# Attention with a gated unit behind it: the factor leaves the maxima before their transpose and meets them behind it, and products of the same columns are issued apart

## The chip, the cores and the metric

The program runs on one core of a Trainium2 chip, as one launch. The metric is the device time of the launch in microseconds. A core has five engines that work in parallel, each through its own instructions in order: TensorE (PE in the profile; its weight loads are PEld), VectorE (DVE), ScalarE (ACT), GpSimd (POOL) and SyncE (SP), which here issues the transfers between memories. Matrix products are written to PSUM (eight banks of 128 rows by 512 fp32 numbers); everything else lies in SBUF.

## What is computed

The inputs are q, k and v of 8 batches and 8 heads, 1152 positions, 64 numbers a head. Queries are averaged in pairs, so 576 query rows meet 1152 keys. The reference, cut to what matters:

```python
q_pool = q.reshape(B, H, S // 2, 2, D).mean(axis=3)
scores = scale * np.matmul(q_pool, k.transpose(0, 1, 3, 2))
scores = scores - np.max(scores, axis=-1, keepdims=True)
attn = np.exp(scores)
attn = attn / (np.sum(attn, axis=-1, keepdims=True) + 1e-09)
x = np.matmul(attn, v)                       # heads side by side: 512 wide
h = np.maximum(x @ w_in, 0.0)
u, v = h[..., :512], h[..., 512:]            # v is normalised over its row
gated = u * (einsum(w_spatial, normalised v) + b_spatial)
return gated @ w_out
```

## The kernel before

**Numbers in two halves.** Products run on 16-bit numbers, and each fp32 operand is split into a high and a low half, scaled by powers of two (`scales`, lines 340 to 357). A score is `khh` times `qhl` (the high half of k against both halves of q, 128 rows deep) plus `KL` times `X` (the low half of k against the high half of q). `KL` and `X` are 66 rows deep: rows 64 and 65 of `X` hold the row's maximum, as two halves, and those of `KL` hold -2^15, so the second product also takes the maximum off.

**Pairs of heads.** The work goes by 32 pairs of heads. For pair i there are four strands, each written as a generator that stops at `yield`:

- `prep(i)` (line 535) loads and splits q and k. It computes the scales `s` and `r`, from these `esc` (the factor of the exponent, line 551, on ACT) and `lnp` (lines 554 to 558, on DVE): log(64) / ESC times the product of the two scales, cut off at 2^29. `lnp` is the same in all 128 rows, since `scales` sums over the rows with a matrix of ones.
- `maxima(i)` (line 594) multiplies q and k once more for the maxima alone: nine groups of 128 query rows, three products of 384 keys each (line 617, or 608 for the group of tails), and one DVE reduction for each (line 623). Its PSUM banks come from the pool `ps_m` (two banks, tile `pm`), and, while no gated unit is under way, in turn from `ps_w` (tile `pw`).
- `shift` (line 631), twice in each `maxima`, for five groups and for four: the three maxima of a group become one (line 635), `lnp` is taken off (636), the 128 x 5 numbers are transposed by PE into a bank of `ps_m` (640), split into two halves divided by 2^15 (642, 643), and sent by two transfers on SP's queue to the two rows of `X` (648).
- `attention(i)` (line 785) goes through 18 steps. Each makes one tile of 128 keys by 512 query rows: two products (793, 794), the exponent on ACT out of PSUM (799), and on POOL the low half of the result, both in SBUF (811). The exponent is kept as fp32; its upper 16 bits are read as bf16, and the rest is stored over the lower 16 bits as fp16. Two steps later `values` (line 699) multiplies the tile with the values: for each of four blocks of 128 query rows, the upper half times the high half of v with a column of ones (713, 65 columns), the upper half times the low half of v (717, 64 columns, into the first 64 of the same columns), and then four times the rest times the high half (722). `tail_tile` (line 801) does the 64 query rows that are left over for each head: four or five blocks of keys, for each one product of line 793 and one of 794 into the same 64 columns, four tiles for each pair of heads.

**The gated unit.** After every second batch a `gated_unit` (line 831) for 1152 rows runs between the steps of the following pairs; its products are 512 columns wide. The last one runs alone at the end. In the first pairs no unit is there yet, and the weights are loaded and split instead (`load_weights`, line 401).

**The order.** The strands are advanced at fixed rates (lines 1101 to 1120), but this gives only a first order. At the end `Order.pin` (line 183) goes through the whole program with a cost for each instruction (`cost`, line 146), keeps what depends on what, and chooses for each engine which instruction comes next: the one that is ready first by its due time, and of those the earliest written. It also has a term for DVE operations that read only SBUF while POOL works on SBUF (`two_from_sbuf`, line 178): they are taken to wait for each other. The order so found is pinned by a dependency from each instruction to the one before it on its engine. Products into one PSUM tile keep their written order. So an edit of a few instructions can move others.

Of the kernel before, what the change touches and what calls it, by code (L numbers as in the profile page):

```python
# [16 lines left out]
AF = mybir.ActivationFunctionType  # L17
ALU = mybir.AluOpType
# [8 lines left out]
MROW = 2.0 ** 15  # L27

PEXP = 2.0 ** 6
# [232 lines left out]
def attn_sgu_kernel(ctx: ExitStack, tc: tile.TileContext, qT, kT, v, w_in, w_spT, b_sp, w_out, out):  # L262
    nc = tc.nc
    P = 128
# [10 lines left out]
    TAIL = S - MAIN  # L275
    S2 = 2 * S
    NT = S2 // P
    KR = D + 2
    ESC = 0.5 / D ** 0.5
# [85 lines left out]
    def square_sum(acc, src, junk):  # L365
        nc.scalar.activation(junk, src, AF.Square, bias=0.0, scale=1.0, accum_out=acc)
# [168 lines left out]
    def prep(i):  # L535
        st = state[i]
        kt, qt = st["kt"], st["qt"]
        X, KL, khh, qhl = (x[i % NSET] for x in (xq, klo, khi, qhi))
        k0 = kt.rearrange("p (c k) -> p c k", k=P)
        q0, q1 = qt[:, 0:S], qt[:, S:]  # L540
        st.update(qhl=qhl, khh=khh, X=X, KL=KL)
        nc.gpsimd.tensor_add(q0, q0, q1)
        sq = sm.tile([P, 2], F32, name="sq", bufs=2)
        junk = KL[:, 0].rearrange("p c k -> p (c k)")
        square_sum(sq[:, 0:1], kt, junk)
        yield
        square_sum(sq[:, 1:2], q0, junk[:, :S])
        yield
        s, r = yield from scales(sq, "qk", math.log2(ESC) / 2)
        esc = sm.tile([P, 1], F32, name="esc", bufs=NSET)  # L550
        nc.scalar.activation(esc, r[:, 0:1], AF.Copy, bias=0.0, scale=r[:, 1:2])


        lnp = sm.tile([P, 1], F32, name="lnp", bufs=2)
        nc.vector.scalar_tensor_tensor(
            out=lnp, in0=s[:, 0:1], scalar=math.log(PEXP) / ESC, in1=s[:, 1:2], op0=ALU.mult, op1=ALU.mult
        )
        nc.vector.tensor_scalar_min(lnp, lnp, 2.0 ** 29)
        st.update(esc=esc, lnp=lnp)
        s_k, s_q = s[:, 0:1], s[:, 1:2]  # L560
        yield

        lower, upper = slice(0, D), slice(D, P)
        head(X[:, 0], q0, s_q)
        rest(qhl[:, 1], q0, s_q, X[:, 0])
        yield
        nc.sync.dma_start(out=qhl[lower, 0], in_=X[lower, 0])
        nc.sync.dma_start(out=qhl[upper, 0], in_=qhl[lower, 1])
        for h, (a, rows) in enumerate(((MAIN, lower), (0, upper))):
            nc.sync.dma_start(out=qd[i % 2][rows, h], in_=X[rows, 0, a : a + TAIL])  # L570
        kn = st["kn"] = ld.tile([P, NC, P], F16, name="kn")
        for a, z in ((0, 5), (5, NC)):
            if i < 8:
                head(kn[:, a:z], k0[:, a:z], s_k)
                yield
                rest(KL[:, 0, a:z], k0[:, a:z], s_k, kn[:, a:z])
            else:
                nc.scalar.activation(k0[:, a:z], k0[:, a:z], AF.Copy, bias=0.0, scale=s_k)
                yield
                nc.scalar.activation(kn[:, a:z], k0[:, a:z], AF.Copy, bias=0.0, scale=1.0)  # L580
                nc.gpsimd.tensor_sub(KL[:, 0, a:z], k0[:, a:z], kn[:, a:z])
            yield
        nc.sync.dma_start(out=khh[lower, 0], in_=kn[lower])
        nc.sync.dma_start(out=khh[upper, 0], in_=kn[lower])
        nc.sync.dma_start(out=qhl[lower, 1], in_=X[upper, 0])
        nc.sync.dma_start(out=khh[lower, 1], in_=kn[upper])
        nc.sync.dma_start(out=khh[upper, 1], in_=kn[upper])
        nc.sync.dma_start(out=X[lower, 1], in_=X[upper, 0])
        nc.sync.dma_start(out=KL[lower, 1], in_=KL[upper, 0])
        nc.sync.dma_start(out=KL[D:KR, 0], in_=KL[D:KR, 1])  # L590
        yield
# [39 lines left out]
    def shift(st, mt, a, z):  # L631
        X = st["X"]
        n = z - a
        mx = sm.tile([P, NT], F32, name="mx", bufs=2)
        nc.vector.reduce_max(out=mx[:, :n], in_=mt[:, a:z], axis=AX.X)
        nc.vector.tensor_scalar_sub(mx[:, :n], mx[:, :n], st["lnp"])
        yield
        yield
        pt = ps_m.tile([P, 512], F32, name="pm")
        nc.tensor.transpose(out=pt[:n, :P], in_=mx[:, :n], identity=ident)  # L640
        mr = sm.tile([NT, 2, P], F16, name="mr", bufs=2)
        nc.vector.tensor_scalar_mul(mr[:n, 0], pt[:n, :P], 1.0 / MROW)
        nc.vector.scalar_tensor_tensor(
            out=mr[:n, 1], in0=pt[:n, :P], scalar=1.0 / MROW, in1=mr[:n, 0], op0=ALU.mult, op1=ALU.subtract
        )
        for r in range(2):
            rows = X[D + r : D + r + 1].rearrange("p h s -> p (h s)")
            nc.sync.dma_start(out=rows[:, a * P : z * P], in_=mr[:n, r])
        yield
# [3 lines left out]
    TAILS = (slice(MAIN, S), slice(0, TAIL))  # L653
# [45 lines left out]
    def values(i, k):  # L699


        st = state[i]
        h, c = divmod(k, NC)
        if c == 0:
            st["o"] = ps_o.tile([P, MAIN], F32, name="o")
        o = st["o"][:, : 4 * D1].rearrange("p (t d) -> p t d", d=D1)
        pt = st["pt"][k]
        top = pt.bitcast(BF16)[:, 1::2]
        rst = pt.bitcast(F16)[:, 0::2]
        vp = vps[i % 2][:, h, c]  # L710
        for t in range(4):
            cols = slice(t * P, (t + 1) * P)
            nc.tensor.matmul(  # L713
                o[:, t], lhsT=top[:, cols], rhs=vp[:, D : D + D1], start=c == 0 and t == 0, stop=False,
                skip_group_check=True,
            )
            nc.tensor.matmul(  # L717
                o[:, t, 0:D], lhsT=top[:, cols], rhs=vp[:, 0:D], start=False, stop=False, skip_group_check=True
            )
        for t in range(4):  # L720
            cols = slice(t * P, (t + 1) * P)
            nc.tensor.matmul(  # L722
                o[:, t], lhsT=rst[:, cols], rhs=vp[:, D : D + D1], start=False, stop=c == NC - 1,
                skip_group_check=True,
            )
        if c == NC - 1:
            if h == 0:
                st["xm"] = wk.tile([P, 4, P], F32, name="xm")
            r = inverse(o[:, :, D], "den")
            nc.vector.tensor_tensor(  # L730
                out=st["xm"][:, :, h * D : (h + 1) * D], in0=o[:, :, 0:D],
                in1=r.unsqueeze(2).to_broadcast([P, 4, D]), op=ALU.mult,
            )
            if h == 1:
                later.append([2, lambda: turn_main(i)])
# [49 lines left out]
    def attention(i):  # L785

        st = state[i]
        qhl, khh, X, KL, esc = (st[n] for n in ("qhl", "khh", "X", "KL", "esc"))
        ptl = pt_.tile([P, NC, 2, TAIL], F32, name="ptl")
        st.update(ptl=ptl, pt=[])  # L790

        def products(o, c, h, q):
            nc.tensor.matmul(o, lhsT=khh[:, h, c, :], rhs=qhl[:, h, q], start=True, stop=False)  # L793
            nc.tensor.matmul(o, lhsT=KL[0:KR, h, c, :], rhs=X[0:KR, h, q], start=False, stop=True)  # L794

        def main_tile(pt, c, h):
            ps = ps_s.tile([P, MAIN], F32, name="pss")
            products(ps, c, h, MAINS[h])
            nc.scalar.activation(pt, ps, AF.Exp, bias=0.0, scale=esc)  # L799

        def tail_tile(h, n):
            ps = ps_s.tile([P, MAIN], F32, name="pss")
            a, z = CUT[n], CUT[n + 1]
            for c in range(a, z):
                products(ps[:, (c - a) * TAIL : (c - a + 1) * TAIL], c, h, TAILS[h])
            o = ps[:, : (z - a) * TAIL].rearrange("p (c s) -> p c s", s=TAIL)
            nc.scalar.activation(ptl[:, a:z, h], o, AF.Exp, bias=0.0, scale=esc)  # L807

        def split(t):

            nc.gpsimd.tensor_sub(t.bitcast(F16)[..., 0::2], t, t.bitcast(BF16)[..., 1::2])  # L811

        for k in range(STEPS):
            h, c = divmod(k, NC)
            st["pt"].append(pp.tile([P, MAIN], F32, name="pt"))
            main_tile(st["pt"][k], c, h)
            split(st["pt"][k])
            yield
            todo.append((i, k))
            turn()  # L820
            yield
            if k in (1, 2, 3, 4):
                tail_tile((k - 1) % 2, (k - 1) // 2)
                yield
            if k == TAIL_SPLIT:
                split(ptl.rearrange("p c h s -> p c (h s)"))
            if k == TAIL_AT:
                tail_values(i)
# [347 lines left out]
```

## Time and profile before

| | |
|---|---|
| Time, median of three runs | 1245.7 us (1244.05 to 1246.76) |
| Profiled execution, its own time | 1241.88 us |
| Span, first to last instruction | 1240.1 us, mean granted clock 0.979 |
| Instructions | 34103 |
| Busy: PE, DVE, ACT, POOL | 94%, 76%, 71%, 70% of the span |
| Transfers | 126.70 MB, mean 102 GB/s |

The profile shows one execution. A row of a group reads: line of the kernel, engine, operation, tile written <- tiles read, shapes, count, then the busy time in us and the mean of one in ns, then the idle time of the engine just before them and what ended it. A row in order of time begins with the start in us and the duration in us. A matrix product's row includes the way through the array, so several overlap, and the distance of two starts says what one costs in a stream.

### The profile page before, as it was taken

Reading aid. Unit: us, or ns where it says so; the run is one execution under the profiler, and the core shown is the slowest. Engines: PE = TensorE matmul, PEld = TensorE weight load, DVE = VectorE, ACT = ScalarE, POOL = GpSimd, SP = SyncE. Lnnn points to the kernel's source line nnn. Section 1 sums busy time; section 2 is a strip of 40 time slices with the busy share of each in tenths; the row PEclk is TensorE's granted clock in tenths of the full one; section 3 lists DMA queues with packets and bytes.
Section 4 is the critical chain, followed back from the end, with each engine's and each line's share of the span. In section 5 each row is a group of like instructions: output and inputs, shape, how many; then the busy total and the mean of one; then the engine's idle time right before and its main releaser. Section 6 shows DMA issues by size and latency. Waiting matters only on the chain.

```text
span 1240.1 us, 34103 instructions
## 1 busy us (share of the span) xinstructions
PE 1165.3 (94%) x13632; PEld 732.9 (59%) x13632; DVE 941.6 (76%) x2219; ACT 885.1 (71%) x1627; POOL 872.4 (70%) x750
## 2 busy tenths in 40 slices
PE   3878879789999999999999999999999999999998
PEld 1555556556666666566666666666665666665454
DVE  5689999998878777876679777876669867841644
ACT  4677669778977787868677887768777786754333
POOL 2768969799878777778787777778877776774000
PEclk9879899899999999999999999999999999999999
DMA  5454364336333533155323432246332321110002
GB/s 186 161 167 137 90 199 120 110 90 198 92 109 78 147 112 104 53 137 165 106 74 93 131 95 68 74 128 186 109 91 74 90 70 50 33 44 36 1 1 77
DMA packets 62335, 126.70 MB, mean 102 GB/s; under 512 B 13728, under 2 KB 21920, under 8 KB 61664
## 3 DMA queue, kind: packets, MB, share of 16 engines
q1 hardware_dynamic: 62176, 124.52, 34.1%
q8 instruction: 107, 1.75, 0.6%
q14 instruction: 52, 0.43, 0.1%
HBM read 81.20 MB, written 9.44 MB: 73 GB/s over the span
## 4 chain that ended last, share of the span: by engine, by line
PE 70%; DVE 13%; ACT 3%; issue 2%; POOL 2%; DMA 1%; ACTq 0%; DVEq 0%; SPq 0%; POOLq 0%
PE pss L793 8%; PE pss L794 8%; PE pm L617 7%; PE pw L868 6%; PE pw L973 6%; PE pw L1016 6%; DVE mt L623 5%; PE pw L932 5%; PE o L713 4%; PE o L722 4%; PE o L717 4%; ACT pt L799 1%; PE pss L868 1%; PE pss L973 1%; DVE vv L372 1%
## 5 line engine op out<-in xcount | busy, mean ns | idle before, releaser
L811 POOL TENSOR_TENSOR pt<-pt 128x512 f16<-128x512 f32 x576 | 637.1, 1123 | 206.4 <-ACT pt L799 204.7
L799 ACT ACTIVATE pt<-pss,esc 128x512 f32<-128x512 f32 x576 | 387.1, 686 | 164.3 <-PE pss L794 122.4
L623 DVE TENSOR_REDUCE mt<-pm 128x1 f32<-128x384 f32 x733 | 385.7, 547 | 60.6 <-PE pm L617 52.4
L793 PE MATMUL pss<-qhi,khi 128*128 128x64 f16 (+1 forms) x1152 | 270.7, 289 | 13.5 <-ACT pt L799 11.2
L794 PE MATMUL pss<-xq,klo 66*128 66x64 f16 (+1 forms) x1152 | 275.8, 290 | 1.5 <-DMA xq<-mr 1.5
L713 PE MATMUL o<-vp,pt 128*128 128x65 f16 x2304 | 229.6, 196 | 0.0
L717 PE MATMUL o<-vp,pt 128*128 128x64 f16 x2304 | 227.6, 194 | 0.0
L617 PE MATMUL pm<-khi,qhi 128*128 128x384 f16 x655 | 206.0, 331 | 14.5 <-DVE mt L623 8.1
L713 PEld LDWEIGHTS <-pt 128*128 128x128 bf16 x2304 | 179.9, 99 | 46.6 <-issue 6.3
L717 PEld LDWEIGHTS <-pt 128*128 128x128 bf16 x2304 | 169.4, 99 | 31.7 <-issue 2.4
L722 PE MATMUL o<-vp,pt 128*128 128x65 f16 x2304 | 172.2, 195 | 0.9 <-POOL pt L811 0.7
L722 PEld LDWEIGHTS <-pt 128*128 128x128 f16 x2304 | 121.6, 99 | 26.2 <-POOL pt L811 4.0
L794 PEld LDWEIGHTS <-klo 66*128 66x128 f16 x1152 | 98.3, 99 | 51.5 <-issue 22.4
L617 PEld LDWEIGHTS <-qhi 128*128 128x128 f16 x768 | 74.7, 99 | 83.3 <-issue 36.2
L793 PEld LDWEIGHTS <-khi 128*128 128x128 f16 x1152 | 99.8, 99 | 30.7 <-issue 7.3
L868 PE MATMUL pw<-wi_h,xg 128*128 128x512 f16 x240 | 89.0, 378 | 0.0
L811 POOL TENSOR_TENSOR ptl<-ptl 128x1152 f16<-128x1152 f32 x32 | 71.3, 2230 | 19.6 <-ACT ptl L807 19.5
L807 ACT ACTIVATE ptl<-pss,esc 128x256 f32<-128x256 f32 (+1 forms) x128 | 63.7, 498 | 29.8 <-PE pss L794 29.4
L932 PE MATMUL pw<-xg,wi_h 128*128 128x512 f16 (+1 forms) x336 | 82.8, 325 | 0.0
L973 PE MATMUL pw<-ws_h,vv 128*128 128x512 f16 x216 | 80.5, 379 | 0.3 <-DVE u L983 0.3
L1016 PE MATMUL pw<-wo_h,vv 128*128 128x512 f16 x216 | 79.7, 379 | 0.8 <-DVE vv L372 0.8
L623 DVE TENSOR_REDUCE mt<-pw 128x1 f32<-128x384 f32 x131 | 70.1, 543 | 11.0 <-PE pw L617 10.5
(190 smaller groups left out, 2335.4 us busy)
## 6 DMA issues: line engine op xcount, KB each, us to landing
vt<-in_v_dram SPq DMA_DIRECT2D x56, 576.0 KB
qt<-in_qT_dram SPq DMA_DIRECT2D x32, 576.0 KB
kt<-in_kT_dram SPq DMA_DIRECT2D x32, 576.0 KB
khi<-kn SPq DMA_DIRECT2D x128, 144.0 KB
out_dram<-row SPq DMA_DIRECT2D x24, 256.0 KB
qhi<-xq SPq DMA_DIRECT2D x64, 72.0 KB
klo<-klo SPq DMA_DIRECT2D x32, 144.0 KB
vv<-in_w_in_dram SPq DMA_DIRECT2D x4, 1024.0 KB
```

The lines of the kernel that those rows point to most:

```text
L617: nc.tensor.matmul(pm[:, :W], lhsT=qhl[:, h, c0 : c0 + P], rhs=khh[:, h, n * NB : (n + 1) * NB, :], start=True, stop=True,)
L623: nc.vector.reduce_max(out=mt[:, t, n : n + 1], in_=pm[:, :W], axis=AX.X)
L713: nc.tensor.matmul(o[:, t], lhsT=top[:, cols], rhs=vp[:, D : D + D1], start=c == 0 and t == 0, stop=False, skip_group_check=True,)
L717: nc.tensor.matmul(o[:, t, 0:D], lhsT=top[:, cols], rhs=vp[:, 0:D], start=False, stop=False, skip_group_check=True)
L722: nc.tensor.matmul(o[:, t], lhsT=rst[:, cols], rhs=vp[:, D : D + D1], start=False, stop=c == NC - 1, skip_group_check=True,)
L793: nc.tensor.matmul(o, lhsT=khh[:, h, c, :], rhs=qhl[:, h, q], start=True, stop=False)
L794: nc.tensor.matmul(o, lhsT=KL[0:KR, h, c, :], rhs=X[0:KR, h, q], start=False, stop=True)
L799: nc.scalar.activation(pt, ps, AF.Exp, bias=0.0, scale=esc)
L811: nc.gpsimd.tensor_sub(t.bitcast(F16)[..., 0::2], t, t.bitcast(BF16)[..., 1::2])
L868: nc.tensor.matmul(ph, lhsT=xa[:, cc, c0 : c0 + P], rhs=wa[:, cc, DH:DF], start=n == 0, stop=n == 3 * NCC - 1,)
L973: nc.tensor.matmul(pv, lhsT=l, rhs=r[:, 0:MAIN], **fl)
L1016: nc.tensor.matmul(py, lhsT=ga[:, fc, c0 : c0 + P], rhs=wa[:, fc, :], start=m == 0, stop=m == end - 1)
```

## The change

Four edits. (1) `lnp` is formed by one ACT copy with a scale and one DVE operation (times log(64) / ESC, cut off at 2^29) in place of two DVE operations. (2) `lnp` is no longer taken off the 128 x 5 maxima in SBUF. Behind the transpose, one DVE operation takes it off in place in PSUM and divides by 2^15; the scalar is read from the first five (or four) rows of `lnp`. (3) The two halves are then made by a copy and a subtraction in place of a multiplication and a multiply-and-subtract. (4) In `values` the four products of line 717 come behind the four of line 713, and in `tail_tile` the products of the low half come behind all those of the high half; there only the first product of the bank carries the start flag and only the last the stop flag.

```diff
         lnp = sm.tile([P, 1], F32, name="lnp", bufs=2)
-        nc.vector.scalar_tensor_tensor(
-            out=lnp, in0=s[:, 0:1], scalar=math.log(PEXP) / ESC, in1=s[:, 1:2], op0=ALU.mult, op1=ALU.mult
+        nc.scalar.activation(lnp, s[:, 0:1], AF.Copy, bias=0.0, scale=s[:, 1:2])
+        nc.vector.tensor_scalar(
+            out=lnp, in0=lnp, scalar1=math.log(PEXP) / ESC, scalar2=2.0 ** 29, op0=ALU.mult, op1=ALU.min
         )
-        nc.vector.tensor_scalar_min(lnp, lnp, 2.0 ** 29)
...
         nc.vector.reduce_max(out=mx[:, :n], in_=mt[:, a:z], axis=AX.X)
-        nc.vector.tensor_scalar_sub(mx[:, :n], mx[:, :n], st["lnp"])
         yield
         yield
         pt = ps_m.tile([P, 512], F32, name="pm")
         nc.tensor.transpose(out=pt[:n, :P], in_=mx[:, :n], identity=ident)
         mr = sm.tile([NT, 2, P], F16, name="mr", bufs=2)
-        nc.vector.tensor_scalar_mul(mr[:n, 0], pt[:n, :P], 1.0 / MROW)
-        nc.vector.scalar_tensor_tensor(
-            out=mr[:n, 1], in0=pt[:n, :P], scalar=1.0 / MROW, in1=mr[:n, 0], op0=ALU.mult, op1=ALU.subtract
+        m = pt[:n, :P]
+        nc.vector.tensor_scalar(
+            out=m, in0=m, scalar1=st["lnp"][:n], scalar2=1.0 / MROW, op0=ALU.subtract, op1=ALU.mult
         )
+        nc.vector.tensor_copy(out=mr[:n, 0], in_=m)
+        nc.vector.tensor_sub(mr[:n, 1], m, mr[:n, 0])
...
                 o[:, t], lhsT=top[:, cols], rhs=vp[:, D : D + D1], start=c == 0 and t == 0, stop=False,
                 skip_group_check=True,
             )
+        for t in range(4):
+            cols = slice(t * P, (t + 1) * P)
             nc.tensor.matmul(
                 o[:, t, 0:D], lhsT=top[:, cols], rhs=vp[:, 0:D], start=False, stop=False, skip_group_check=True
             )
...
-            for c in range(a, z):
-                products(ps[:, (c - a) * TAIL : (c - a + 1) * TAIL], c, h, TAILS[h])
+            cols = [ps[:, (c - a) * TAIL : (c - a + 1) * TAIL] for c in range(a, z)]
+            for c, x in zip(range(a, z), cols):
+                nc.tensor.matmul(
+                    x, lhsT=khh[:, h, c, :], rhs=qhl[:, h, TAILS[h]], start=c == a, stop=False, skip_group_check=True
+                )
+            for c, x in zip(range(a, z), cols):
+                nc.tensor.matmul(
+                    x, lhsT=KL[0:KR, h, c, :], rhs=X[0:KR, h, TAILS[h]], start=False, stop=c == z - 1,
+                    skip_group_check=True,
+                )
```

## The prediction

> **What bounds the kernel now.** I read the totals of the engines first, then the busy time of every engine in stretches of the span, because a share over the whole hides two different stages.
>
> ```profile
> PE 1165.3 (94%) x13632; PEld 732.9 (59%) x13632; DVE 941.6 (76%) x2219; ACT 885.1 (71%) x1627; POOL 872.4 (70%) x750
> 60.00:290.00 230.00, 193.12 (x2505) 129.51 (x2506) 215.19 (x466) 173.82 (x310) 189.40 (x147) 0.92 0.46 135
> 290.00:1140.00 850.00, 839.96 (x10201) 536.87 (x10200) 639.24 (x1550) 641.45 (x1182) 653.10 (x568) 1.00 0.34 97
> ```
>
> In the last two rows the columns are PE, weight load, DVE, ACT and POOL, then the granted clock. From 60 to 290 us DVE is busy 215.2 of 230 us, 94%, and PE 84%. From 290 to 1140 us PE is busy 840.0 of 850 us, 99%, and DVE 75%. I call 0 to 290 us stage A and the second stretch stage B: time taken off DVE is worth something in A, time taken off PE in B. The waits of PE in stage A (total us, times, longest), and one row of the weight load's waits in B, say how much:
>
> ```profile
> PE pw L617 <- DVE mt L623: 13.1, 21, 1.9
> PE pss L793 <- ACT pt L799: 11.2, 14, 2.2
> PE pm L345 <- ACT klo L366: 8.2, 1, 8.2
> PE pw L617 <- DMA khi<-kn: 7.4, 1, 7.4
> PE pm L617 <- DVE mt L623: 3.9, 6, 1.2
> PE pm L640 <- DVE lnp L558: 3.5, 6, 1.7
> PE pss L794 <- DMA xq<-mr: 1.5, 2, 0.9
> PE pm L640 <- DVE mx L636: 1.3, 3, 0.5
> PE pm L617 <- DVE mr L643: 1.0, 1, 1.0
> PEld pm L640 <- DVE mx L636: 2.1, 4, 0.7
> ```
>
> The nine rows of stage A sum to 51.1 us. 22.8 us of it (13.1 + 3.9 + 3.5 + 1.3 + 1.0), 45%, is PE waiting for DVE, 19.4 us for ACT, 8.9 us for DMAs.
>
> **The subtraction that goes (DVE).** It works on 128x5 or 128x4 numbers, and yet it is long. First its minimum, median and maximum over the 64 of the run; then the DVE groups of stage A that the edit touches; then two of them in order of time, one beside a POOL instruction and one without.
>
> ```profile
> L636 DVE TENSOR_SCALAR mx<-mx,lnp x64: 214/766/1290, 25.0 to 1102.0; 128x5 f32<-128x5 f32 x32, 128x4 f32<-128x4 f32 x32
> L636 DVE TENSOR_SCALAR mx<-mx,lnp 128x5 f32<-128x5 f32 (+1 forms) x18 | 12.2, 677 | 0.0
> L642 DVE TENSOR_SCALAR mr<-pm 5x128 f16<-5x128 f32 (+1 forms) x18 | 5.0, 277 | 6.8 <-PE pm L640 6.5
> L643 DVE SCALAR_TENSOR_TENSOR mr<-pm,mr 5x128 f16<-5x128 f32 (+1 forms) x18 | 4.9, 271 | 0.0
> L555 DVE SCALAR_TENSOR_TENSOR lnp<-qks 128x1 f32<-128x1 f32 x10 | 4.7, 469 | 0.1
> L558 DVE TENSOR_SCALAR lnp<-lnp 128x1 f32<-128x1 f32 x10 | 1.4, 145 | 0.1
> 533.69 1.04 POOL L811 TENSOR_TENSOR pt<-pt 128x512 f16<-128x512 f32 x1
> 534.04 0.71 DVE L636 TENSOR_SCALAR mx<-mx,lnp 128x4 f32<-128x4 f32 x1
> 380.32 0.23 DVE L636 TENSOR_SCALAR mx<-mx,lnp 128x5 f32<-128x5 f32 x1
> ```
>
> The POOL subtraction ends at 533.69 + 1.04 = 534.73 us, L636 at 534.75: it is held until POOL is through. Without such a neighbour it takes 0.23 us. L555, which also reads only SBUF, shows the same spread in its mean (469 ns for one number a row); L642 and L643, which read PSUM, and L558 do not. So the edit takes away 12.2 + 4.7 + 1.4 = 18.3 us of DVE in stage A, most of it held time.
>
> **What DVE gets instead.** The new factor costs an ACT copy and one DVE operation of L558's form: 10 x 145 ns = 1.45 us in A; were it held like L555, 4.7 us. After the transpose there are three operations on 5x128 numbers in place of two. The nearest rows:
>
> ```profile
> L980 DVE SCALAR_TENSOR_TENSOR pw<-pw,r_v,b_bc 128x512 f32<-128x512 f32 x27 | 20.3, 754 | 25.6 <-PE pw L974 13.5 <-ACT vt L523 6.9 <-PE pss L974 2.7
> L980 DVE SCALAR_TENSOR_TENSOR pw<-pw,r_v,b_bc 128x64 f32<-128x64 f32 x27 | 7.6, 281 | 0.0
> L771 DVE TENSOR_SCALAR xt<-pm,dent 64x64 f32<-64x64 f32 x64 | 17.9, 279 | 0.6
> 500.38 0.28 DVE L642 TENSOR_SCALAR mr<-pm 4x128 f16<-4x128 f32 x1
> 500.72 0.27 DVE L643 SCALAR_TENSOR_TENSOR mr<-pm,mr 4x128 f16<-4x128 f32 x1
> L551 ACT ACTIVATE esc<-qkr x32: 277/294/333, 9.2 to 1051.2; 128x1 f32<-128x1 f32 x32
> ```
>
> In-place PSUM work exists (L980): (754 - 281) / 448 = 1.06 ns an element. The subtraction with a scalar read from a tile is L771 with 64 elements more: 279 + 68 = 347 ns. The copy is taken as L642 (277), the last subtraction as L643 (271). A dependent pair has 500.72 - 500.66 = 0.06 us between, once more than before. Sum: 347 + 277 + 271 + 60 - (277 + 271) = 407 ns more for each of the 18, 7.3 us. Lower bound: the first as cheap as L642 and the copy half of that, 277 + 140 + 271 + 60 - 548 = 200 ns, 3.6 us. Upper bound: all three at 347 with two gaps, 347 x 3 + 120 - 548 = 613 ns, 11.0 us. Net in stage A: -18.3 + 1.45 + 7.3 = **-9.5 us of DVE**, between -18.3 + 1.45 + 3.6 = -13.3 and -18.3 + 4.7 + 11.0 = -2.6.
>
> How much of it reaches the end lies between 45% (DVE's part of PE's waits) and 94% (DVE's busy share); I take 70%, the middle: **-6.7 us**. In stage B the same swap happens under a PE that is 99% busy and is worth only the waits of the transposes: half of 2.1 us, **-1.0 us**; bounds 0 and 2.1.
>
> The VectorE page (VectorE: DVE Perf Modes, section "The TRN2 errata — SBUF-src ops pay a fixed extra latency per instruction") of the Trainium skill speaks against the swap: it gives 58 cycles plus the elements for SBUF to SBUF and 120 plus the elements out of PSUM, at 0.96 GHz. By that page an estimate is 63 cycles, 66 ns, removed, and 248 cycles, 258 ns, added, so DVE would lose 64 x 0.19 = 12 us. The trace disagrees for the removed one: 214 ns at the least and 766 in the median.
>
> **Edits at no cost.** The ACT copy is one more of L551's kind, 294 ns, 2.9 us in stage A, under an ACT that is busy 174 of 230 us. SP issues the same two transfers for each group of rows, later by the 407 ns and earlier by what L636 took; only two waits of 1.5 us in all ever ended on them, and the tail products that need these rows now come behind the ones that don't. The PSUM bank of the transpose is held 0.4 us longer; the other bank covers it, as the one wait of 1.0 us for L643 shows. Uncovered, it would be 18 x 0.4 = 7 us in A, the same DVE time that is counted above.
>
> **The matrix products.** Nothing is added or removed; the question is whether two products into the same columns cost more behind each other. Three groups of stage B, each eight L713/L717 in alternation and four L722 into four different columns, and a tail tile of ten alternating products:
>
> ```profile
> 600.67 0.19 PE L713 MATMUL o<-vp,pt 128*128 128x65 f16 x1
> 600.92 0.29 PE L722 MATMUL o<-vp,pt 128*128 128x65 f16 x4
> 601.04 0.38 PE L793 MATMUL pss<-qhi,khi 128*128 128x512 f16 x1
> 605.13 0.19 PE L713 MATMUL o<-vp,pt 128*128 128x65 f16 x1
> 605.37 0.28 PE L722 MATMUL o<-vp,pt 128*128 128x65 f16 x4
> 605.50 0.38 PE L793 MATMUL pss<-qhi,khi 128*128 128x512 f16 x1
> 501.11 0.28 PE L722 MATMUL o<-vp,pt 128*128 128x65 f16 x4
> 501.22 0.20 PE L713 MATMUL o<-vp,pt 128*128 128x65 f16 x1
> 501.47 0.38 PE L794 MATMUL pss<-xq,klo 66*128 66x512 f16 x1
> 610.49 0.19 PE L793 MATMUL pss<-qhi,khi 128*128 128x64 f16 x1
> 610.81 0.33 PE L617 MATMUL pm<-khi,qhi 128*128 128x384 f16 x1
> ```
>
> Same columns in turn: (0.25 + 0.24 + 0.25) / 24 = 30.8 ns. Different columns: (0.12 + 0.13 + 0.11) / 12 = 30.0 ns. The single groups go from 3.7 ns for the new order (501) to 2.5 ns against it (605). Over 576 groups of eight, 0.8 ns is 3.7 us; the times are rounded to 10 ns, so I take less than half, **-1.5 us**, bounds -6 and +2 (a third and more of these groups lie in A or beside other waits). The tail's ten take 0.32 us, 32 ns each; the cheapest row above is 27.5 (0.11 / 4). The new order can save 0 to 4.5 ns for each of 36 products in the (64 - 18) / 2 = 23 pairs of heads whose maxima lie in B, 0 to 3.7 us; nearest to the first groups, whose difference was small, **-1.0 us**.
>
> **Sum.** -6.7 - 1.0 - 1.5 - 1.0 = -10.2 us. The profiled execution took 1241.9 us (span 1240.1) and would take 1231.7; the median of the runs lies 3.8 us above it, so **1235.5 us** there.
>
> **The rivals.**
> *More than that.* The copy is cheap and DVE sets nearly all of stage A: 13.3 x 0.94 = 12.5, with 2.1, 3.7 and 3.7 us for the rest: -22.0, 1223.7 us. For it speaks DVE's 94%; against it that ACT and DMAs end more than half of PE's waits.
> *Nearly nothing.* The three operations are dear and POOL (189 of 230), ACT and PE are right behind DVE in A: 2.6 x 0.45 = 1.2 us, products unchanged: 1244.5 us. For it speaks that four engines are over 75% busy there, and that the program's planner orders all queues anew for changed costs, for better or worse.
> *Slower: DVE stops for the factor.* DVE now needs a result of ACT, and behind the waiting operation stand L623's reductions, which free the banks that PE waits for. The trace has such waits of DVE for ACT:
>
> ```profile
> DVE stt L878 <- ACT vv L876: 28.9, 16, 2.7
> ```
>
> That is 1.8 us each. Ten of them in stage A cost 18 us at 94%, 17: -10.2 + 17 = +6.8, 1252.5 us. It decides from a wait of 1.1 us for each factor (10.2 / (10 x 0.94)). Against it: the planner puts the DVE operation where it expects ACT to be done, and reductions can go ahead of it.
> *Slower: the held time was spare.* If DVE would have waited elsewhere instead, L636 is worth 214 ns and L555 no more than L558: 18 x 0.21 + 10 x 0.145 = 5.3 us saved against 7.3 added, +2.0, and with unchanged products 1247.7 us. The 94% speaks against it. It is the way in which the page's figures would come true.
>
> **How the numbers follow.** The forecast has 0.53, with its own range 1230 to 1241; more than that 0.12; nearly nothing 0.20; DVE stops 0.09; spare time 0.06. The range 1226 to 1247.5 leaves out the stops, half of the last and a third of the first rival. Within 0.2% (2.5 us), about what a measurement can tell, lie over half of "nearly nothing", half of the last and a little of the forecast, 0.16; slower are the stops and the other halves, 0.14; faster is the rest, 0.70.
>
> **What would show it.** Right: no L636, the lnp operation near 145 ns, DVE's busy time lower by about 30 us (64 x (0.68 - 0.41) + 32 x 0.47), stage A shorter by 5 to 9 us, the new in-place operation at 280 to 350 ns. Wrong: rows of DVE waiting for ACT's lnp with over 1 us each; a new first wait of L617; a stage A of the old length with an idle DVE; or eight values products that take clearly less than 0.24 us, which would make the products the larger part.

## The result and the profile after

The changed kernel takes 1227.4 us (1226.1 to 1227.9) against 1244.9 us of the kernel before: a ratio of 0.9861 with a 95% interval of 0.9838 to 0.9884, or -17.3 us (-14.4 to -20.2). The forecast was -10.2 us. The direction and nearly every price were right; the gain in stage B was larger than the sum had it. The profiled execution took 1227.1 us, its span is 1225.3 us, against 1241.9 and 1240.1, a difference of 14.8 us. The four executions behind the 1244.9 us lie high: in 75 more of the kernel before, run beside the experiments below, the median is 1242.4 us. So about 15 us is the better figure for the gain.

The totals of the changed kernel, and its stretches in the same columns as before (PE, weight load, DVE, ACT, POOL, granted clock):

```profile
PE 1153.0 (94%) x13632; PEld 725.7 (59%) x13632; DVE 906.2 (74%) x2187; ACT 889.2 (73%) x1659; POOL 875.8 (71%) x750
60.00:290.00 230.00, 194.38 (x2590) 128.91 (x2587) 209.18 (x466) 182.61 (x332) 196.63 (x150) 0.95 0.48 142
290.00:1140.00 850.00, 840.67 (x10203) 536.07 (x10201) 615.47 (x1532) 640.51 (x1198) 649.42 (x565) 1.00 0.34 96
```

DVE's busy time falls by 941.6 - 906.2 = 35.4 us (about 30 were expected). The first stretch holds more work of PE, ACT and POOL than before in the same 230 us, and the granted clock in it is 0.95 in place of 0.92.

The DVE and ACT groups that are new or moved, of the first 290 us, and the spread of the in-place operation and of the factor's DVE operation over the whole run (minimum, median, maximum):

```profile
L642 DVE TENSOR_SCALAR pm<-pm,lnp 5x128 f32<-5x128 f32 (+1 forms) x18 | 6.2, 342 | 8.5 <-PE pm L639 8.4
L645 DVE CAST mr<-pm 5x128 f16<-5x128 f32 (+1 forms) x18 | 4.9, 272 | 0.0
L646 DVE TENSOR_TENSOR mr<-pm,mr 5x128 f16<-5x128 f32 (+1 forms) x18 | 4.9, 271 | 0.1
L555 ACT ACTIVATE lnp<-qks 128x1 f32<-128x1 f32 x10 | 2.8, 285 | 0.2 <-DVE qks L356 0.2
L556 DVE TENSOR_SCALAR lnp<-lnp 128x1 f32<-128x1 f32 x10 | 1.4, 143 | 1.0 <-ACT lnp L555 1.0
L642 DVE TENSOR_SCALAR pm<-pm,lnp x64: 330/347/348, 28.6 to 1089.1; 5x128 f32<-5x128 f32 x32, 4x128 f32<-4x128 f32 x32
L556 DVE TENSOR_SCALAR lnp<-lnp x32: 131/144/155, 9.7 to 1036.5; 128x1 f32<-128x1 f32 x32
```

347 ns in the median for the in-place operation (worked out: 347), 272 for the copy (277), 271 for the subtraction (271), 143 for the factor's operation (145), 285 for ACT's (294). None of them spreads (the copy and the last subtraction take 268 to 279 ns each over the whole run): no operation is held by POOL any more in the shift. DVE waits for ACT's factor for 1.0 us in these 290 us, so the rival in which DVE stops for the factor did not come about.

Who made PE idle in the changed kernel from 0 to 290 us, some of the rows (total us, times, longest):

```profile
PE pss L796 <- ACT pt L802: 12.8, 12, 2.1
PE pw L617 <- DVE mt L623: 9.0, 16, 2.0
PE pm L617 <- DVE mt L623: 5.3, 5, 1.6
PE pw L617 <- DVE mx L635: 2.5, 1, 2.5
PE pm L639 <- DVE mx L635: 0.9, 2, 0.5
```

The same from 290 to 1140 us, first of the changed kernel, then of the kernel before, all rows of both:

```profile
PE pw L1027 <- DVE vv L372: 3.9, 4, 1.4
PE o L725 <- POOL pt L822: 2.4, 3, 1.1
PE pm L747 <- DVE xm L733: 1.0, 2, 0.5
PE pm L617 <- DVE rs L911: 1.0, 3, 0.3
PE pm L617 <- DVE mt L623: 0.5, 2, 0.4
```

```profile
PE pm L617 <- DVE mt L623: 4.2, 9, 1.1
PE pm L617 <- DVE xt L771: 2.5, 3, 0.8
PE pm L617 <- DVE rs L900: 1.0, 3, 0.4
PE pw L1016 <- DVE vv L372: 0.8, 3, 0.3
PE pw L973 <- DVE u L983: 0.3, 2, 0.2
PE pm L640 <- DVE mx L636: 0.3, 2, 0.2
PE o L722 <- POOL pt L811: 0.2, 1, 0.2
```

In the first stage the waits of the transposes fall from 4.8 to 0.9 us. In the second the waits of L617 for a reduction (4.2) and for xt (2.5) all but vanish, but waits for L372, POOL and xm come up in their place: all rows together fall only from 9.3 to 8.8 us. This view leaves out short waits, since the row of a product runs on while the product is on its way through the array; the distances of starts, used below, count them too.

To see where a gain lies I use two landmarks of each trace: the start of the ninth pair's first exponent (until then there is no gated unit under way) and the stretch from it to the start of the last exponent. The last column is the time between the first pair and the ninth for which the granted clock was 0.5.

| kernel | ratio to before (95%) | ninth pair starts, us | ninth to last pair, us | at half clock, us |
|---|---|---|---|---|
| before | 1 | 286.7 | 848.0 | 44.7 |
| the change | 0.9861 (0.9838 to 0.9884) | 280.0 | 839.9 | 33.0 |
| factor and shift alone | 0.9886 (0.9858 to 0.9913) | 276.8 | 840.8 | 17.1 |
| products alone | 0.9989 (0.9966 to 1.0012) | 287.4 | 847.3 | 43.0 |
| subtraction twice | 1.0078 (1.0056 to 1.0099) | 296.6 | 849.2 | 49.4 |
| before, planner 60 | 0.9992 (0.9974 to 1.0010) | 290.3 | 848.7 | 55.3 |
| before, planner 45 | 1.0011 (0.9995 to 1.0027) | 281.8 | 850.4 | 29.7 |
| lnp alone | 0.9986 (0.9964 to 1.0008) | 281.4 | 850.7 | 35.4 |
| shift alone | 1.0028 (1.0013 to 1.0044) | 294.0 | 844.8 | 55.5 |
| shift alone, planner 60 | 1.0037 (1.0019 to 1.0055) | 292.0 | 849.3 | 48.3 |
| shift alone, planner 45 | 0.9977 (0.9959 to 0.9994) | 292.6 | 843.7 | 55.9 |
| the change, planner 60 | 0.9881 (0.9853 to 0.9910) | 276.5 | 843.5 | 31.6 |
| the change, planner 45 | 0.9906 (0.9884 to 0.9928) | 276.0 | 850.0 | 34.3 |
| factor as a bias | 0.9838 (0.9816 to 0.9860) | 278.8 | 837.6 | 36.0 |

The landmarks are of one profiled execution each, the ratios of all. So the change gains 6.7 us up to the ninth pair, the same as the forecast's -6.7, and 848.0 - 839.9 = 8.1 us behind it, where the forecast had 1.0 + 2.5 = 3.5.

The time up to the ninth pair, of the kernel before and of the changed one, in the columns used above:

```profile
0.00:286.72 286.72, 226.12 (x2810) 147.14 (x2810) 249.03 (x546) 204.85 (x373) 216.04 (x180) 0.91 0.47 143
0.00:280.02 280.02, 220.91 (x2780) 143.13 (x2781) 238.30 (x537) 207.62 (x384) 216.37 (x179) 0.93 0.49 146
```

DVE is busy 10.7 us less there (forecast: 9.5). But of PE's 6.7 us only 1.5 are waits (60.6 us not busy against 59.1); 5.2 us are busy time. The products up to there are the same work: 181.9 and 181.8 us if all ran at full clock (counted by their columns, as explained at the second experiment). They got shorter because PE ran 11.7 us less at half clock. At 0.33 us for each us at half clock, worked out in the last section, that is 3.9 of the 6.7 us. The forecast had no term for the clock.

### The profile page after: what moved, and what is told of

It reads as the page before. It is cut to its first block, busy times and chain, and to the rows that moved or that the text cites. A ratio compares the mean times of both kernels' runs of the same rounds, so it can differ in the third digit from the quotient of the medians.

```text
span 1225.3 us, 34090 instructions
## 1 busy us (share of the span) xinstructions
PE 1153.0 (94%) x13632; PEld 725.7 (59%) x13632; DVE 906.2 (74%) x2187; ACT 889.2 (73%) x1659; POOL 875.8 (71%) x750
## 4 chain that ended last, share of the span: by engine, by line
PE 72%; DVE 8%; ACT 2%; POOL 1%; issue 1%; DMA 1%; SPq 1%; ACTq 0%; DVEq 0%; POOLq 0%
PE pss L797 7%; PE pss L796 7%; PE pm L617 7%; PE pw L984 6%; PE pw L879 6%; PE pw L1027 6%; PE pw L943 5%; PE o L725 4%; PE o L714 4%; PE o L720 4%; DVE mt L623 3%; DVE vv L372 2%; PE pss L879 1%; PE pss L984 1%; PE pss L1027 1%
## 5 line engine op out<-in xcount | busy, mean ns | idle before, releaser
L796 PE MATMUL pss<-qhi,khi 128*128 128x512 f16 x576 | 220.5, 384 | 13.9 <-ACT pt L802 12.8
L797 PE MATMUL pss<-xq,klo 66*128 66x512 f16 x576 | 221.1, 385 | 1.3 <-DMA xq<-mr 1.3
L617 PE MATMUL pm<-khi,qhi 128*128 128x384 f16 x655 | 205.5, 330 | 10.9 <-DVE mt L623 5.9
L714 PEld LDWEIGHTS <-pt 128*128 128x128 bf16 x2304 | 132.2, 99 | 69.1 <-issue 4.7
L725 PE MATMUL o<-vp,pt 128*128 128x65 f16 x2304 | 169.6, 194 | 2.5 <-POOL pt L822 2.4
L714 PE MATMUL o<-vp,pt 128*128 128x65 f16 x2304 | 170.8, 194 | 0.2
L720 PE MATMUL o<-vp,pt 128*128 128x64 f16 x2304 | 168.3, 194 | 0.0
L617 PEld LDWEIGHTS <-qhi 128*128 128x128 f16 x768 | 73.8, 99 | 81.9 <-issue 38.0
L720 PEld LDWEIGHTS <-pt 128*128 128x128 bf16 x2304 | 112.3, 99 | 3.3 <-issue 0.5
L797 PEld LDWEIGHTS <-klo 66*128 66x128 f16 x576 | 57.1, 99 | 43.3 <-issue 17.4
L623 DVE TENSOR_REDUCE mt<-pw 128x1 f32<-128x384 f32 x131 | 69.2, 541 | 11.1 <-PE pw L617 10.7
L796 PEld LDWEIGHTS <-khi 128*128 128x128 f16 x576 | 56.7, 99 | 21.0 <-issue 3.6
```

Source lines behind the costliest of these rows:

```text
L617: nc.tensor.matmul(pm[:, :W], lhsT=qhl[:, h, c0 : c0 + P], rhs=khh[:, h, n * NB : (n + 1) * NB, :], start=True, stop=True,)
L623: nc.vector.reduce_max(out=mt[:, t, n : n + 1], in_=pm[:, :W], axis=AX.X)
L714: nc.tensor.matmul(o[:, t], lhsT=top[:, cols], rhs=vp[:, D : D + D1], start=c == 0 and t == 0, stop=False, skip_group_check=True,)
L720: nc.tensor.matmul(o[:, t, 0:D], lhsT=top[:, cols], rhs=vp[:, 0:D], start=False, stop=False, skip_group_check=True)
L725: nc.tensor.matmul(o[:, t], lhsT=rst[:, cols], rhs=vp[:, D : D + D1], start=False, stop=c == NC - 1, skip_group_check=True,)
```

## The experiments

**Factor and shift alone, and products alone.** The change is cut in two: edits (1) to (3) in one kernel, the order of the products in the other.

```diff
 e1: lnp, shift as in the change; values, tail_tile as before
 e2: lnp, shift as before; values, tail_tile as in the change
```

> The first three edits alone (factor and shift), the products as before. My theory, by the prediction's steps: 6.7 us less in stage A and 1.0 us less in stage B, about 1237 us, with L636 gone and the span shorter by about 7 us at the start of the ninth pair. Rival 1 (the products carry most of what stage B gained, 8.1 us between the ninth pair and the end in the changed kernel): the same 1237 us, and the ninth pair early by 6 to 7 us, but no further gain behind it. Rival 2 (taking the held operations away also shortens PE's waits for DVE in stage B): about 1232 us, with 4 to 6 us gained behind the ninth pair.

> The fourth edit alone (the order of the products in values and in the tail tiles), the factor as before. My theory: -2.5 us, about 1242 us, nothing of it in stage A. Rival 1 (same columns behind each other cost more than I took): -5 to -8 us, 1237 to 1240 us, all of it behind the ninth pair and in even steps from pair to pair. Rival 2 (the gain in stage B comes from DVE): no difference, 1245 us.

The first three edits alone take 1229.2 us against 1241.9, -14.2 us by the ratio (-10.8 to -17.6): nearly all of the change's gain. 9.9 us of the profiled execution lie before the ninth pair and 848.0 - 840.8 = 7.2 behind it. That execution is the fastest of its six: 1224.8 us at a granted clock of 0.990, where their medians are 1229.2 and 0.981. So up to 4.4 of the 9.9 us may be missing in a usual execution. The 7.2 us speak for the second rival, that with less work on DVE PE waits less in stage B too; the other orders below qualify this. PE's waits of that kernel from 290 to 1140 us, its three largest and the reductions:

```profile
PE pw L1017 <- DVE vv L372: 3.7, 4, 1.4
PE pm L745 <- DVE xm L731: 1.0, 2, 0.5
PE pm L617 <- DVE rs L901: 0.9, 3, 0.3
...
PE pm L617 <- DVE mt L623: 0.3, 1, 0.3
```

The products alone give 1240.8 against 1241.9 us, and the interval holds 1: no difference can be told, and the two landmarks move by +0.7 and -0.7 us. Yet the products themselves do get cheaper. Eight of them took 0.24 to 0.25 us before; in the changed kernel, four at a time (three groups in a row, then a tail tile of eight):

```profile
591.93 0.28 PE L714 MATMUL o<-vp,pt 128*128 128x65 f16 x4
592.06 0.28 PE L720 MATMUL o<-vp,pt 128*128 128x64 f16 x4
592.17 0.29 PE L725 MATMUL o<-vp,pt 128*128 128x65 f16 x4
593.38 0.28 PE L714 MATMUL o<-vp,pt 128*128 128x65 f16 x4
593.50 0.28 PE L720 MATMUL o<-vp,pt 128*128 128x64 f16 x4
593.62 0.29 PE L725 MATMUL o<-vp,pt 128*128 128x65 f16 x4
594.94 0.28 PE L714 MATMUL o<-vp,pt 128*128 128x65 f16 x4
595.06 0.28 PE L720 MATMUL o<-vp,pt 128*128 128x64 f16 x4
595.17 0.28 PE L725 MATMUL o<-vp,pt 128*128 128x65 f16 x4
607.32 0.28 PE L809 MATMUL pss<-qhi,khi 128*128 128x64 f16 x4
607.44 0.28 PE L813 MATMUL pss<-xq,klo 66*128 66x64 f16 x4
607.56 0.33 PE L617 MATMUL pm<-khi,qhi 128*128 128x384 f16 x1
```

Eight products take (0.24 + 0.24 + 0.23) / 24 = 29.6 ns each, where the three groups before had 30.8, and the tail's eight (0.24 / 8) 30 in place of 32. Over the whole stretch from the ninth to the last pair I took every distance between two starts less (columns / 2.4 + 2.5) ns, and split what is left. This line fits the usual distances of the stretch: 56 ns for 128 columns, 162 for 384, 216 for 512; the few fp32 products count as 110 ns each, their usual distance. The result: distances that are too long by under 8 ns sum to 13.5 us before and 10.2 with the products alone; those too long by more, the waits, to 19.3 and 22.7. So 3.3 us were saved at the products, more than the 2.5 forecast, and 3.4 us came back as waits. The same pair shows between the first three edits alone (13.6 and 12.8) and the whole change (10.3 and 15.5). That the time saved turns into waits because DVE and ACT set the pace next is argued, not shown: other orders shift the waits by as much.

**The subtraction twice.** The held time itself, doubled:

```diff
         nc.vector.tensor_scalar_sub(mx[:, :n], mx[:, :n], st["lnp"])
+        mj = sm.tile([P, NT], F32, name="mj", bufs=2)
+        nc.vector.tensor_scalar_sub(mj[:, :n], mx[:, :n], st["lnp"])
```

> The kernel before, with the subtraction of line 636 done a second time into a tile that nobody reads: one more held DVE operation in each of the 64 shifts, nothing else changed. If the time for which DVE is held is on the path in stage A, as the prediction has it: 18 more operations of 0.2 to 1.2 us there, at 0.7 of their time some 3 to 9 us longer, 1248 to 1254 us, and little in stage B. If the held time was spare (the last rival of the prediction): no difference within 2.5 us. If DVE's held time also costs PE in stage B: over 10 us longer.

```profile
L638 DVE TENSOR_SCALAR mj<-mx,lnp 128x5 f32<-128x5 f32 (+1 forms) x17 | 13.4, 785 | 0.0
L638 DVE TENSOR_SCALAR mj<-mx,lnp x64: 215/963/1324, 25.5 to 1114.1; 128x5 f32<-128x5 f32 x32, 128x4 f32<-128x4 f32 x32
```

It takes 1252.6 against 1241.9 us, +9.7 (+7.0 to +12.3), and in the profiled execution 9.9 us lie before the ninth pair. 13.4 us of added DVE time there became 9.9 us: 74%, beside the 70% that I had put between 45 and 94. A part of it is again the clock, with 49.4 us at half clock in place of 44.7. The rival in which the held time was spare is out. Behind the ninth pair 47 more of these operations make DVE 32 us busier and cost 849.2 - 848.0 = 1.2 us. So in stage B held time that is added is nearly free, and the 7.2 us that went when it was taken away are not simply its reverse.

That POOL is what holds them shows in the order of time: of the 64 doubles, 51 start while a POOL operation runs, and every one of these ends 22 to 30 ns behind that operation; the 9 that meet no POOL operation take 231 ns at most. In the changed kernel 54 of the 64 in-place operations start while POOL works, and none takes over 348 ns.

The SBUF page (SBUF — State Buffer, "Who interferes with whom") of the Trainium skill says that one of DVE's two port pairs is shared with GpSimd as an exclusive lock, held for a whole instruction, and that only DVE operations with two SBUF inputs or in a two-port mode take it. The traces agree: L636 and its double run to 1290 and 1324 ns beside POOL, the operations out of PSUM stay within 20 ns.

**Another order of the same work.** The planner's allowance between engines is changed by a few ns; nothing else.

```diff
-                    x = end + (140 if lane[m] == "Pool" else 54)
+                    x = end + (140 if lane[m] == "Pool" else 60)
```

> The kernel before with one number of the planner changed: 60 in place of 54 ns between an instruction's end and its reader on another engine. No instruction is added, removed or changed, but their order on the engines comes out another way. It shows how much time another order makes by itself. My theory: within 3 us of before, 1242 to 1248 us. Rival (part of the change's gain is an accident of the new order): a shift of 5 us or more, of either sign.

> The kernel before with the same number of the planner changed the other way, 45 in place of 54 ns: another order of the same instructions. If the gain from the ninth to the last pair is an accident of the order, this stretch (848.0 us before, 848.7 with 60 ns) comes out several us shorter or longer; if not, within 1.5 us, and the time within 3 us of before.

For the kernel before, another order makes no difference that can be told (0.9992 and 1.0011), and its stage B stays within 848.0 to 850.4 us.

> The whole change with the planner's number at 60: does its gain hold in another order? If the gain comes from the work that is saved: 1225 to 1231 us, and the stretch from the ninth to the last pair 838 to 843 us. If a good order gave a part of it: 1232 us or more.

> The whole change with the planner's number at 45. If the gain comes from the work that is saved: 1225 to 1231 us again, with the ninth to the last pair in 838 to 843 us; if a good order gave a part of it: 1232 us or more here or with 60.

For the changed kernel it does. Up to the ninth pair both orders are as good as the one that was measured (276.5 and 276.0 us), so that gain belongs to the change. Behind it they give 843.5 and 850.0 us where the change had 839.9. With 60 the time is again about 15 us below before, with 45 only 11.7 us (8.9 to 14.4). The last one lies between what was expected: 1231.7 us is just under the 1232 put down for luck, but 850.0 us is far outside 838 to 843.

Over three orders stage B takes 844.5 us on average with the change and 849.0 without, 4.6 us less. By the same distances as above, most of this is found again: those too long by under 8 ns sum to 10.2 or 10.3 us in each of the three orders with the change and 13.4 or 13.5 without, so 3.3 us are the products'. The waits sum to 15.5, 19.1 and 23.3 us with the change (54, 60, 45 ns) and to 19.3, 20.1 and 21.3 without: 0.9 us less on average, where single orders lie 8 us apart. So three orders do not show that the swap on DVE gains anything in stage B, and they do not exclude a few us. With 54 ns the kernels without held subtraction and factor operation do wait less there (12.8, 15.5, and 13.6 with the factor as a bias), but these runs cannot tell that from luck of this order: the first three edits alone were not run in another one.

**The edits one at a time.**

```diff
 e5: only lnp by ACT and one DVE operation; the subtraction stays in SBUF
 e6: only the shift; lnp by two DVE operations as before
 e9, e10: as e6, with 60 and 45 in the planner
```

> The first edit alone: the factor lnp by an ACT copy and one DVE operation, everything else as before. In the first pairs it takes about 10 x 0.47 us of held DVE time away; at 0.7 of that: -3 us, about 1239 us. If DVE stops for ACT's result: a row of DVE waiting for ACT's lnp and up to 7 us more than before. For the stretch from the ninth to the last pair (848.0 us before, 840.8 with the first three edits): if the two operations of lnp, which stand in front of reductions that PE waits for, are what makes PE wait there, this stretch alone gets shorter by 3 us or more; if it is the shift, it stays within 1 us.

> The second and third edit alone: the factor taken off behind the transpose, lnp formed as before on DVE. By the prediction's terms the first stage loses 12.2 us of held time and gets 7.3 us of PSUM work: -4.9 x 0.7 = -3.4 us; with what the first three edits together showed (-9.9 us by the ninth pair), rather -5 to -7. From the ninth to the last pair: if the shift's held subtraction, with the transposes behind it, is what PE waited for, 841 to 843 us in place of 848.0; if lnp is, 847 to 849.

> The second and third edit alone, as in the run that came out 2.8 us slower than before, with the planner's number at 60 in place of 54 ns: the same instructions in another order. If that loss belongs to the edit, it is there again, 1244 to 1247 us. If it is an accident of the order in the first pairs, the time comes out at 1236 to 1241 us, since the stretch from the ninth to the last pair, 844.8 us in place of 848.0, stays short.

> The same with 45 ns. If the loss is the edit's: 1244 to 1247 us again. If it is the order's: below 1242 us in at least one of the two, and the two differ by over 2 us.

The factor's edit alone is 1.7 us faster by the ratio, with 1 in the interval. Its ninth pair starts 5.3 us early, and distances that are 5.6 us too long in the tenth pair take it back: one wait of 3.2 us for a held L636, and right behind it 3.4 us at half clock. The shift's edit alone is slower, by 3.5 us (1.6 to 5.5). Its ninth pair starts 7.3 us late in the profiled execution, where I had expected -3.4 or better, and its stage B is 3.2 us shorter; but 2 us of both are products that this order issues before the landmark instead of behind it (183.9 us of them by columns up to there, against 181.9). Against the kernel before in the same order, the ninth pair is late by 1.7 us with 60 and by 10.8 us with 45. In time the edit loses again with 60 (+4.6 us, 2.4 to 6.8) and gains with 45 (-2.9 us, 0.7 to 5.1). One is below 1242 us and the two differ by 7 us, which was put down beforehand as the sign that the order makes the loss, and not the edit. Together with the factor's edit the same shift gains. What the trace shows of the loss: the stretch of 60 to 290 us of the kernel with the shift alone, then two of its groups, then the first of them in the kernel before.

```profile
60.00:290.00 230.00, 191.17 (x2440) 128.78 (x2437) 209.63 (x455) 169.78 (x304) 185.03 (x142) 0.90 0.45 133
```

```profile
L384 DVE TENSOR_SCALAR u<-vv 128x1024 int32<-128x1024 int32 x6 | 8.7, 1446 | 0.0
L555 DVE SCALAR_TENSOR_TENSOR lnp<-qks 128x1 f32<-128x1 f32 x10 | 5.7, 572 | 0.0
```

```profile
L384 DVE TENSOR_SCALAR u<-vv 128x1024 int32<-128x1024 int32 x6 | 5.6, 926 | 0.0
```

In the first 290 us DVE's preparation of the weights and its factor operation are held for longer than before, and from 60 to 290 us DVE is busy no longer than before (209.6 against 215.2 us), but idle longer; some of the held time only moves to other operations on SBUF (L384 is 3.1 us longer, L555 1.0); and PE's clock is lower, 0.90 against 0.92, with 55.5 us at half clock in place of 44.7. The clock goes with the whole loss: over all executions the mean granted clock is 0.975 with the shift alone and 0.981 before, which is 63 us at half clock against 48 (the span times 1 - clock, doubled), and at 0.33 us each the 15 us make 5 us. Why this order leaves PE idle in such stretches more often is left open: the orders of the two kernels differ in too many places to name one.

**The factor as a bias.**

```diff
-        m = pt[:n, :P]
-        nc.vector.tensor_scalar(
-            out=m, in0=m, scalar1=st["lnp"][:n], scalar2=1.0 / MROW, op0=ALU.subtract, op1=ALU.mult
+        nc.vector.tensor_scalar_mul(mr[:n, 0], pt[:n, :P], 1.0 / MROW)
+        nc.vector.scalar_tensor_tensor(
+            out=mr[:n, 1], in0=pt[:n, :P], scalar=1.0 / MROW, in1=mr[:n, 0], op0=ALU.mult, op1=ALU.subtract
         )
-        nc.vector.tensor_copy(out=mr[:n, 0], in_=m)
-        nc.vector.tensor_sub(mr[:n, 1], m, mr[:n, 0])
...
-            nc.scalar.activation(pt, ps, AF.Exp, bias=0.0, scale=esc)
+            nc.scalar.activation(pt, ps, AF.Exp, bias=bias_p, scale=esc)
```

> The factor left out of the maxima altogether: it is added in the exponent instead, as a bias of log(64) read from a column of 128 rows, so that lnp, the in-place operation and one of the three operations behind the transpose are gone (the two halves are made as before the change); the cut-off at 2^29 is left out with it. The products stand as in the changed kernel. If DVE's time is still on the path in the first pairs: 18 x 0.4 + 10 x 0.15 = 8.7 us less DVE there than in the changed kernel, at 0.7 of it -6 us: about 1221 us. If ACT pays for a bias from memory (704 exponents), each by 50 ns or more, ACT takes 35 us more and the time rises again: 1230 us or above.

```profile
PE 1154.3 (94%) x13632; PEld 723.4 (59%) x13632; DVE 879.7 (72%) x2092; ACT 943.7 (77%) x1627; POOL 876.0 (72%) x750
L797 ACT ACTIVATE pt<-pss,bias_p,esc 128x512 f32<-128x512 f32 x576 | 439.2, 777 | 124.4 <-PE pss L792 89.0 <-POOL pt L817 16.2 <-PE o L720 14.1
```

1223.1 us, a ratio of 0.9838 (0.9816 to 0.9860): the lowest of all, but its interval overlaps the change's. DVE is busy 906.2 - 879.7 = 26.5 us less than in the changed kernel, and ACT 943.7 - 889.2 = 54.5 us more, because each exponent now takes 777 ns (687 in the changed kernel). So ACT pays more than the 35 us named above, and yet the time does not rise to 1230 us: ACT, busy 77% of the span, had the room.

## Why the prediction was right, and where its sizes were off

**The removed subtraction, right.** That L636 is long because POOL holds it, that its time is on the path in the first stage, and at about 70%: doubled, it became 74%. (The 45% that bounded the share from below stood on nine rows; with all rows of 0 to 290 us it is 27.3 of 58.1 us, 47%.) **What DVE gets instead, right**: each price within 4%, DVE's waits for the factor 1.3 us in the whole run by the view of waits. **Stage A, -6.7 us, right in direction and size, by luck to the tenth**: 6.7 in the profiled execution. Averaged over three orders it is more: the ninth pair starts at 277.5 us with the change and at 286.3 without, -8.8. And 3 to 4 us of either figure go with the clock (33.0 us at half clock on average in place of 43.2), for which the sum had no term; what DVE's waits gave by themselves is nearer to 3 to 5 us. The 70% are a share that these runs bear out with the clock in it.

**Stage B, -1.0 us, too small for the order that was measured.** This is the term that missed. I let the swap count there only for the waits of the transposes (bounds 0 and 2.1), because PE was busy at 99%. In this order the waits fell by 6.5 us with the first three edits and by 3.8 with the whole change. Waits that I left out stood in the profile: those of L617 for reductions and for L771, 6.7 us in two rows, are waits for the same DVE queue out of which the swap took 639.2 - 615.5 = 23.8 us. They went down to 0.5 us and to no row at all, but others came up in their place. Over three orders the waits fell by 0.9 us, which is the term as forecast; the rest of the miss is luck of the order, as far as three orders can tell.

**The products, -2.5 us, right at the products.** They got 3.3 us cheaper in stage B, in every order. The kernel with their edit alone did not get faster; over three orders of the whole change the 3.3 us do show in the stretch.

**The planner, no term.** The sum took the order of the queues as given. Changing 54 to 60 or 45 ns moved the changed kernel's stage B by 3.6 and 10.1 us.

**The rivals.** "More than that" came nearest in size (-22 forecast, -17.3 measured), by another term than its own: the copy was not cheap, and DVE did not set 94% of stage A. Against the 75 further executions, where the gain is about 15 us, the forecast itself is the nearer one. "Nearly nothing" is out by the result, the stop for the factor by its 1.3 us of waits, the spare held time by the doubled subtraction. The estimate from the figures of the VectorE page of the Trainium skill (VectorE: DVE Perf Modes, "The TRN2 errata"), DVE losing 12 us, is out too: DVE's busy time fell by 35.4 us.

## What to carry to other kernels

An operation on five numbers can cost 0.7 us when both it and a neighbour on another engine read SBUF; look at minimum, median and maximum of small operations, and try the long ones on operands in PSUM, even where that makes three operations of two. Here that paid together with the factor's edit, and not by itself. Where one engine is busy at 99%, look at all its waits before the gain behind it is put at nearly nothing, and afterwards at their sum: single rows vanished here and others took their place. Where a planner orders the queues, measure the edit in two or three orders before crediting it with the last few us: here they spread by 10 us in one stage. And read the granted clock of each execution before comparing two landmarks.

## What the runs showed of the hardware that was not expected

PE's granted clock drops to one half in stretches of 3.4 us and multiples of it (3.4, 6.8, 10.2, 13.7, 17.1 us in the records), between the first pair and the ninth for 17 to 56 us in total; behind the ninth pair one trace has one such stretch (the factor's edit alone), the others none up to their last products. Four kernels with the same DVE work (before, both other orders, products alone) needed from the first pair to the ninth 254.2, 257.7, 249.2 and 254.7 us with 44.7, 55.3, 29.7 and 43.0 us at half clock: (257.7 - 249.2) / (55.3 - 29.7) = 0.33 us for each us at half clock, and the other two lie within about 1 us of that line. The 75 executions of the kernel before bear it out: their granted clocks lie between 0.975 and 0.985, their times fall with the clock (correlation 0.83), by 0.34 us for each us less at half clock. Most of the spread between executions goes with the clock.

What sets it off can be read from the traces. The stretches of one trace all start on one grid of 3.41 us. I cut each trace from 35 to 1130 us into the pieces of its grid and took PE's busy share in each. Over the 14 traces, all 63 pieces at full clock in which PE is busy under 48% are followed by half clock, 48 of the 121 between 48 and 63%, and none of the 4141 above. Inside the half-clock stretches products of 512 columns usually start 426 ns apart, elsewhere in the first 290 us 218 ns. So the clock falls after PE has had too little to do for 3.4 us, and costs PE time itself. The TensorE page (TensorE: Matmul & The Clock Gate, "Part 1: The HAM clock gate") of the Trainium skill gives a free-running window of 3.4 us after whose idleness the clock is halved; the lengths and the grid here agree with the window, but it need not be idle throughout: no wait of PE between the first pair and the ninth is longer than 2.5 us. An engine that saves PE its idle moments in such a stage may thus gain twice.
